# The written-out opening of a spectral-filter plus gated-MLP kernel, in another order

## The chip, the cores and the metric

One core of a Trainium2 chip runs the whole problem in one launch. Its engines are TensorE (PE: matmuls, with weight loads beside them), VectorE (DVE), ScalarE (ACT), GpSimd (POOL) and SyncE (SP), which issues the DMA transfers. Each takes its own instructions strictly in the order in which they stand in its queue, and waits at one until the semaphores that it names are reached. The metric is the device time of one execution in microseconds (us).

## The reference

The input `x` is 2048 tokens by 448 features, float32. The output is `x` plus two branches:

```python
xn = _layernorm(x, axis=-1)
A = irfft2(rfft2(xn) * (w_r + 1j * w_i))            # spectral filter over tokens and features
gate, up = x @ W_gate, x @ W_up                     # 448 -> 1792, here with xn for x
B = ((gate * (gate > 0)) * up) @ W_down             # 1792 -> 448
return x + A + B
```

Both branches take the normalised input `xn`.

## The kernel before

The tokens lie in 16 blocks of 128 (block n2), and four blocks make a chunk of 512: chunk 0 is blocks 0, 4, 8 and 12, chunk 2 is blocks 2, 6, 10 and 14. Every float32 operand of a matmul is split in two float16 parts, hi and lo, and a product is three matmuls (hi·hi, lo·hi, hi·lo). A block is normalised by DVE's bn_stats and bn_aggr, a reciprocal square root on ACT (`ln_sd`), three small DVE instructions that sharpen it (`ln_rstd`), and a fourth that makes the bias -mean·r. `ln_xn` writes the normalised block in float32 and `ln_hi` its hi part `tt`; `ln_copy` moves some columns on POOL, `ln_lo` subtracts on DVE. Then the block is transposed to the matmul layout `T`: in chunk 0 by TensorE (`ln_tp`, two groups of tiles a block, into PSUM) with a copy out of PSUM (`ln_ev`), in the other chunks by a transposing DMA (`ln_dma`).

The weights of gate and up come as slabs of 128 output features: slab (f, g), g = 0 gate, 1 up. A slab is loaded by DMA (256 KB, tile `wst`), its squares are summed on ACT (`w_sq`), POOL adds them over the partitions (`w_sum`), two small DVE instructions make a power of two of it (`w_scale`), ACT writes the hi part (`w_hi`) and DVE the lo part (`w_lo`), both into `wt`. A unit (f, chunk) is the 2x10 matmuls of both slabs of f with a chunk (`gu_full`), into two PSUM banks, and four matmuls of half the rows (`gu_halves`); then relu, product, and hi and lo parts of h (L799 to L811). Units of five f's are followed by the product with W_down (L834). The spectral branch is laid between them by a scheduler.

The first part, up to the first two units of chunk 2, is written out by hand: `OPENING` (L30 to L42) is a list of piece names, and each engine gets its instructions in the order in which the names stand. The names are a tag and a block or slab: `lx` load a block, `lw` load the next weight slab, `st` statistics, `sqA rsA` roots of blocks 0 and 4, `sqB rsB` of 8 and 12, `sqC rsC` of chunk 2; `ax` or `xn` normalise on ACT or DVE, `hi`/`hx` hi part from the raw or the normalised block, `cp`, `lo`; `tpA`/`tpB` transposes of a block, `vev`/`aev` the copy out of PSUM by DVE or ACT; `wsq par wsc whi wlo` the steps of a weight slab; `hh lh hl` (f = 0) and `ah bh ch` (f = 1) the matmuls of a slab with one half (256 columns) of chunk 0; `gu`, `hp` the later slabs and half-row matmuls; `re tm gh gl` the steps after a unit; `gz` slabs of chunk 2; `lwd wdq wdp wdsc wdh wdl` the W_down tiles; `warm` and `kw4` matmuls on zeros that nobody reads (`keep_warm`, 21 and 4 of them, 512 columns each).

SP's transfers use eight semaphores in turn, so one can be issued only when the eighth before it has landed.

Of the kernel before, what the change touches and what calls it, by code (L numbers as in the profile page):

```python
# [33 lines left out]
tpB12 wsqW3g0 vevB8 wloW1g0 ah10 wsqW3g1 vevB12 ah01 parW2 ah11 lwd2 wloW1g1 wscW2 bh00 hl11 hl01 lx14 whiW2g0
bh01 hp0 ch10 whiW2g1 lw st2 bh11 st6 re0 wloW2g0 bh10 wsqW4g1 ch00 ch11 tm0 gu2g0 parW3 wscW3 st14 wsqW4g0
whiW3g0 wloW2g1 ch01 ly0 parW4 wscW4 whiW3g1 wloW3g1 lw wsqW5g1 lx10 whiW4g0 wloW3g0 gh0 re1 st10 gu2g1 tm1 hp2
sqC rsC wsqW5g0 xn6 gu3g0 re2 parW5 wscW5 whiW5g0 tm2 wloW4g0 xn10 xn14 hx14 lwd4 hx6 lo6 hi10 whiW5g1 lo10
gu4g0 hx2 wloW5g0 whiW4g1 cp14 xn2 wdq0 gl0 cp10 gu3g1 wloW4g1 lo14 lwd3 wdq4 wdq2 cp2 re3 tm3 cp6 wloW5g1 gh1
# [106 lines left out]
def tile_gfnet_reglu(ctx: ExitStack, tc: tile.TileContext, x, xr, xi, wgu, wd, wf, c_fd, c_fm, c_im, c_row, c_id,  # L145
# [106 lines left out]
    def ln_stats(q, j):  # L252
        n2 = q + 4 * j
        st = ft([128, 6], F32, "bst", 2)
        V.bn_stats(st, xr_t[n2])  # L255
# [1031 lines left out]
```

## Time and profile before

| | us |
|---|---|
| median of 3 runs | 443.69 |
| lowest, highest | 442.72, 444.27 |
| span of the profiled execution, first to last instruction | 440.9 |
| PE busy in it | 435.7 |
| DVE, ACT busy in it | 382.3, 184.5 |

The profiled execution is known by its span alone. The runs' times hold what lies around the span too; their median is 2.8 us above it. A matmul's start is measured and its end is modelled: an own duration of 0.22 us stands for a matmul of 128 columns that lets the next one start after 0.06 us. So the pace is read from the starts.

### The profile page before, as it was taken

How to read it: one execution, taken by the hardware profiler on the slowest of the kernel's cores; microseconds unless marked ns; L12 is line 12 of the kernel's file. 1: busy time of each engine (PE TensorE's matmuls, PEld its weight loads, DVE VectorE, ACT ScalarE, POOL GpSimd, SP SyncE). 2: the span in 40 equal slices, each digit the busy share in tenths (PEclk: the TensorE clock that was granted, in tenths of full speed). 3: DMA queues.
4: the chain of work that ended last, by engine and by line, in shares of the span. 5: the costliest groups of instructions: out<-in, count | busy, mean ns of one | idle time of the engine just before them, and what ended most of it. 6: DMA issues, size and time to landing. Idle time of an engine off the chain costs nothing.

```text
span 440.9 us, 7429 instructions
## 1 busy us (share of the span) xinstructions
PE 435.7 (99%) x2641; PEld 221.9 (50%) x2641; DVE 382.3 (87%) x957; ACT 184.5 (42%) x396; POOL 29.4 (7%) x75
## 2 busy tenths in 40 slices
PE   8999999999999999999999999999999999999996
PEld 3744464554445545444545444444545555555664
DVE  6998496989887879999999999988997989798644
ACT  6995427392457236144023467233113332243220
POOL 3230002011100040000000020000000000000000
PEclk9999999999999999999999999999999999999999
DMA  7929895304111123332220210001111121210212
GB/s 256 301 91 198 269 364 172 70 2 107 59 49 50 47 76 119 94 118 84 86 84 1 84 43 1 0 1 42 44 43 49 54 91 34 72 55 33 89 51 104
DMA packets 37613, 39.55 MB, mean 90 GB/s; under 512 B 16535, under 2 KB 33353, under 8 KB 37577
## 3 DMA queue, kind: packets, MB, share of 16 engines
q1 hardware_dynamic: 37576, 39.09, 29.1%
q8 instruction: 20, 0.33, 0.3%
q14 instruction: 17, 0.13, 0.1%
HBM read 24.38 MB, written 3.67 MB: 64 GB/s over the span
## 4 chain that ended last, share of the span: by engine, by line
PE 90%; DVE 4%; ACT 3%; DMA 1%; issue 1%; SPq 0%; POOL 0%; ACTq 0%
PE bank L757 49%; PE bank L834 27%; PE bank L764 3%; PE fx L648 2%; PE fx L369 2%; PE fx L667 2%; PE fx L406 2%; PE bank L853 2%; ACT wt L699 1%; DMA T<-tt 1%; ACT junk L185 1%; DVE bst L255 1%; DVE wt L703 1%; DMA y<-in_xr 1%; ACT tt L304 1%
## 5 line engine op out<-in xcount | busy, mean ns | idle before, releaser
L757 PE MATMUL bank<-T,wt 128*128 128x512 f16 (+1 forms) x1160 | 252.7, 372 | 0.6 <-DVE T L345 0.5
L757 PEld LDWEIGHTS <-wt 128*128 128x128 f16 x1160 | 110.9, 98 | 127.6 <-issue 7.2
L834 PE MATMUL bank<-wdt,h 128*128 128x448 f16 x624 | 122.4, 352 | 0.0
L834 PEld LDWEIGHTS <-h 128*128 128x128 f16 x624 | 60.5, 98 | 55.1
L799 ACT ACTIVATE g<-bank 128x512 f32<-128x512 f32 x56 | 33.0, 591 | 80.4 <-PE bank L757 45.2
L807 ACT ACTIVATE h<-g 128x512 f16<-128x512 f32 x56 | 35.0, 627 | 70.1 <-DVE g L803 70.0
L803 DVE SCALAR_TENSOR_TENSOR g<-bank,g 128x512 f32<-128x512 f32 x56 | 38.2, 683 | 11.9 <-PE bank L757 6.8
L811 DVE TENSOR_TENSOR h<-g,h 128x512 f16<-128x512 f32 x56 | 38.1, 684 | 6.7 <-ACT h L807 6.4
L840 DVE SCALAR_TENSOR_TENSOR xy<-bank,dsc,xy 128x448 f32<-128x448 f32 x44 | 29.8, 676 | 5.5 <-PE bank L834 5.2
L632 ACT ACTIVATE vt<-y,fsc 128x456 f16<-128x456 f32 x15 | 10.1, 674 | 34.5 <-issue 14.0
L699 ACT ACTIVATE wt<-wst,wsc 128x512 f16<-128x512 f32 x28 | 19.3, 713 | 11.1 <-DVE wsc L195 10.3
L703 DVE SCALAR_TENSOR_TENSOR wt<-wst,wsc,wt 128x512 f16<-128x512 f32 x28 | 20.4, 742 | 0.5 <-ACT wt L699 0.3
L672 DVE SCALAR_TENSOR_TENSOR xy<-fx,fsc,xy 128x448 f32<-128x448 f32 x16 | 10.8, 680 | 10.9 <-PE fx L667 10.9
L188 POOL PARTITION_ALL_REDUCE wm<-wm x15 | 10.5, 697 | 139.9 <-ACT junk L185 136.4
L185 ACT ACTIVATE junk<-wst 128x512 bf16<-128x512 f32 x28 | 17.2, 616 | 0.0
L397 ACT ACTIVATE Xh<-X 128x456 f16<-128x456 f32 x16 | 9.3, 579 | 16.4 <-DVE X L395 9.3
L764 PE MATMUL bank<-T,wt 64*128 64x512 f16 x112 | 15.6, 380 | 0.0
L400 DVE TENSOR_TENSOR Xh<-X,Xh 128x456 f16<-128x456 f32 x16 | 9.8, 624 | 4.9 <-ACT Xh L397 4.9
L648 PE MATMUL fx<-im,vt 128*128 128x128 f16 x192 | 13.3, 219 | 0.0
L667 PEld LDWEIGHTS <-pgh 114*128 114x128 f16 x192 | 10.9, 98 | 3.8 <-issue 0.8
L648 PEld LDWEIGHTS <-vt 128*128 128x128 f16 x192 | 11.6, 98 | 1.3
L406 PE MATMUL fx<-Xh,fm 128*128 128x456 f16 x48 | 12.2, 356 | 0.0
(168 smaller groups left out, 480.1 us busy)
## 6 DMA issues: line engine op xcount, KB each, us to landing
wst<-in_wgu SPq DMA_DIRECT2D x28, 256.0 KB
sw<-y SPq DMA_DIRECT2D x56, 112.2 KB
wf<-in_wf SPq DMA_DIRECT2D x16, 228.0 KB
xy<-in_x SPq DMA_DIRECT2D x16, 224.0 KB
y<-in_xr SPq DMA_DIRECT2D x15, 224.0 KB
out<-xy SPq DMA_DIRECT2D x15, 224.0 KB
wdst<-in_wd SPq DMA_DIRECT2D x14, 224.0 KB
fm<-in_c_fm SPq DMA_DIRECT2D x4, 256.0 KB
```

Source lines behind the costliest of these rows:

```text
L185: A.activation(mt([128, 512], BF16, "junk", 2)[:, 0:src.shape[-1]], src, AF.Square, scale=SQ, accum_out=acc)
L648: P.matmul(o, v[:, h, w], m[:, c, :], start=(i == 0), stop=(i == 2), skip_group_check=True)
L699: A.activation(w[:, 0:4, :], wst[f, g], AF.Copy, scale=wsc[f, g])
L703: V.scalar_tensor_tensor(w[:, 4:8, :], st, sc, w[:, 0:4, :], op0=OP.mult, op1=OP.subtract)
L757: last["P"] = P.matmul(hps[f, q][g][:, cs], wt[f, g][:, a, :], Tq[q][:, b, cs], start=(start and i == 0), stop=(stop and i == len(seq) - 1 ...
L764: m = P.matmul(hps[f, q][g][:, 0:512], wt[f, g][rows, 7, :], Tq[q][rows, b, :], start=start, stop=stop).ins
L799: last["A"] = A.activation(g1s[f, q], hps[f, q][0], AF.Relu, scale=2.0 ** -22).ins
L803: last["V"] = V.scalar_tensor_tensor(g1, hps[f, q][1], 2.0 ** -22, g1, op0=OP.mult, op1=OP.mult).ins
L807: A.activation(ht[f, q][:, 0, :], g1s[f, q], AF.Copy)
L811: V.tensor_tensor(h[:, 1, :], g1s.pop((f, q)), h[:, 0, :], op=OP.subtract)
L834: last["P"] = P.matmul(ps[:, 0:D], ht[f, q][:, a, js], wdt[f][:, b, :], start=(i == 0), stop=(i == n - 1)).ins
L840: last["V"] = V.scalar_tensor_tensor(xy[:, n2, :], dps[n2][:, 0:D], dsc[:, g:g + 1], xy[:, n2, :], op0=OP.mult, op1=OP.add).ins
```

## The change

`OPENING` is written in another order, with a few new pieces, and the code gets what these need:

- `sq0 rs0`, `sq4 rs4`: blocks 0 and 4 have their roots apart, without the bias (`ln_bias`, pieces `nm0`, `nm4`, comes late); `rs` tiles have four buffers for three. Both blocks are normalised on DVE (`xn0`, `xn4`), and ACT makes the hi parts by a plain copy (`hx0`, `hx4`).
- `wsqW0g0` stands ahead of these copies on ACT, and `parW0g0 wscW0g0` follow early.
- The loads stand in another order: first the two blocks, slab W0g0, block 12, slabs W0g1 and W1g0, block 8. `fd_t` (`lfd`) comes among the first 12.
- The first unit's first half is done block by block: `hq lq kq` are 3, 3 and 4 matmuls of 128 columns; 40 matmuls of 128 columns stand for 20 of 256.
- Five of the eight copies out of PSUM are on ACT (`aevA0`, `aevB0`, `aevA8`, `aevA12`, `aevB8`).
- `vh8`, `vh12`, `vh6` make hi parts on DVE straight from the raw block, and `vwW2g0`, `vwW4g1` the hi parts of two weight slabs on DVE.
- The warming matmuls are 15 ahead of the transposes, 5 behind the first six transposes and 1 more.

```diff
-NWARM = 21
...
-OPENING = """lx0 st0 lx4 st4 sqA rsA ax4 hi0 lx8 st8 lx12 xn0 lw cp0 lw lw lw hx4 warm tpA4 st12 tpA0 lo0 lx6 sqB rsB cp4 lo4
-wsqW0g0 tpB0 kw4 tpB4 wsqW0g1 lx2 hi8 parW0g0 wscW0g0 lwd1 whiW0g0 vevA0 parW0g1 wscW0g1 vevA4 hh00 tpA8 whiW0g1
...
+OPENING = """lx0 lx4 lw st0 sq0 st4 sq4 rs0 wsqW0g0 rs4 lx12 xn0 hx0 parW0g0 xn4 wscW0g0 hx4 warm15 lw lw tpA0 st12 lo4 tpA4
+wsqW0g1 cp4 parW0g1 cp0 vevA4 lx8 warm5 tpB4 whiW0g0 aevA0 warm1 lw lo0 hq00 wloW0g0 tpB0 wsqW1g0 lq00 lwd4 wsqW1g1 lw
...
     def ln_sd(q, js=(0, 1, 2, 3)):
-        w = ft([128, 4, 4], F32, "rs", 3)
+        w = ft([128, 4, 4], F32, "rs", 4)
...
+    def ln_bias(q, js):
+        w, m = rsb[q, js[0]]
+        V.scalar_tensor_tensor(w[:, 3], m[:, :, 0], -1.0, w[:, 2], op0=OP.mult, op1=OP.mult)
...
-    def ln_hi(n2, fused=False):
+    def ln_hi(n2, fused=False, eng=None):
...
+        if eng is not None:
+            eng.tensor_scalar(o, xr_t[n2], mean, r, op0=OP.subtract, op1=OP.mult)
+        elif fused:
...
-    def w_hi(f, g):
+    def w_hi(f, g, eng=None):
...
+            eng.tensor_scalar(w[:, 0:4, :], wst[f, g], wsc[f, g], None, op0=OP.mult)
...
+                for j in range(2):
+                    for tag, sq in (("hq", seq1[0:3]), ("lq", seq1[3:6]), ("kq", seq2)):
+                        piece(f"{tag}{g}{j}", gu_full, f, q, (g,), slice(128 * j, 128 * j + 128), tag == "hq" and j == 0,
+                              False, sq)
```

ACT's queue behind its first instruction (`mv` statistics, `rs` roots, `wst` raw weights, `junk,wm` sums of squares, `wt` split weights, `y` and `tt` a block and its hi part, `T` the transposed chunk, `fx` a PSUM bank). Before:

```order
L266 ACTIVATE rs<-mv,eps 128x2
L295 ACTIVATE y_67<-g_127,rs 128x448
L304 ACTIVATE tt_100<-y_66,rs 128x448
L306 ACTIVATE tt_101<-y_67 128x448
L266 ACTIVATE rs<-mv,eps 128x2
L185 ACTIVATE junk,wm<-wst 128x512 x2
L304 ACTIVATE tt_102<-y_68,rs 128x448
L699 ACTIVATE wt<-wst,wsc 128x512 x2
L304 ACTIVATE tt_103<-y_69,rs 128x448
L185 ACTIVATE junk,wm<-wst 128x512 x2
```

Now:

```order
L265 ACTIVATE rs<-mv,eps 128x1 x2
L184 ACTIVATE junk,wm<-wst 128x512
L311 ACTIVATE tt_100<-y_68 128x448
L311 ACTIVATE tt_101<-y_69 128x448
L184 ACTIVATE junk,wm<-wst 128x512
L705 ACTIVATE wt<-wst,wsc 128x512
L348 ACTIVATE T_62<-fx 128x3x128
L184 ACTIVATE junk,wm<-wst 128x512 x2
L705 ACTIVATE wt<-wst,wsc 128x512
L348 ACTIVATE T_62<-fx 128x5x128
```

The two copies into `tt` are fed by DVE's blocks, the first sum of squares stands ahead of them and the second behind, and copies out of PSUM (L348) stand between the steps of the weights.

DVE's queue behind the statistics of blocks 0 and 4. Before:

```order
L258 BN_AGGR mv<-bst 128x2
L271 SCALAR_TENSOR_TENSOR rs<-mv,rs 128x2
L272 SCALAR_TENSOR_TENSOR rs<-rs 128x2
L273 SCALAR_TENSOR_TENSOR rs<-rs 128x2
L275 SCALAR_TENSOR_TENSOR rs<-mv,rs 128x2
L255 BN_STATS bst<-y_68 128x6
L258 BN_AGGR mv<-bst 128x2
L297 TENSOR_SCALAR y_70<-y_66,mv,rs 128x448
L255 BN_STATS bst<-y_69 128x6
L258 BN_AGGR mv<-bst 128x2
```

Now:

```order
L257 BN_AGGR mv<-bst 128x2
L270 SCALAR_TENSOR_TENSOR rs<-mv,rs 128x1
L271 SCALAR_TENSOR_TENSOR rs<-rs 128x1
L272 SCALAR_TENSOR_TENSOR rs<-rs 128x1
L270 SCALAR_TENSOR_TENSOR rs<-mv,rs 128x1
L271 SCALAR_TENSOR_TENSOR rs<-rs 128x1
L272 SCALAR_TENSOR_TENSOR rs<-rs 128x1
L300 TENSOR_SCALAR y_68<-y_66,mv,rs 128x448
L300 TENSOR_SCALAR y_69<-g_123,mv,rs 128x448
L190 TENSOR_SCALAR eg<-wm 128x1
L194 TENSOR_SCALAR wsc<-eg 128x1
```

Two sets of roots, one column wide each, stand where one set of two columns stood; both blocks follow at once, then the scale of the first slab and block 12's statistics.

SP's queue from its start (`in_xr`, `in_xi` blocks, `in_wgu` weight slabs, `in_wd` W_down). Before:

```order
L225 DMA y_66<-in_xr 128x448
L220 DMA g_127<-in_xi 128x512
L225 DMA y_68<-in_xr 128x448
L225 DMA y_69<-in_xr 128x448
L231 DMA wst<-in_wgu 128x512 x4
L225 DMA y_71<-in_xr 128x448
L225 DMA y_72<-in_xr 128x448
L241 DMA wdst<-in_wd 128x448
L214 DMA xy<-in_x 128x448
L231 DMA wst<-in_wgu 128x512 x6
```

Now:

```order
L224 DMA y_66<-in_xr 128x448
L219 DMA g_123<-in_xi 128x512
L230 DMA wst<-in_wgu 128x512
L224 DMA y_67<-in_xr 128x448
L230 DMA wst<-in_wgu 128x512 x2
L224 DMA y_70<-in_xr 128x448
L230 DMA wst<-in_wgu 128x512
L240 DMA wdst<-in_wd 128x448
L230 DMA wst<-in_wgu 128x512 x2
L1104 DMA fd_t<-in_c_fd 128x912
L230 DMA wst<-in_wgu 128x512 x2
L224 DMA y_71<-in_xr 128x448
```

The first weight slab is the third transfer for the fifth, the second slab is the fifth for the sixth.

## Rows read from the trace of the kernel before

**Rows 1.** The page: busy time of each engine, share of the span; PEclk by slice.

```profile
PE 435.7 (99%) x2641; PEld 221.9 (50%) x2641; DVE 382.3 (87%) x957; ACT 184.5 (42%) x396; POOL 29.4 (7%) x75
...
PEclk9999999999999999999999999999999999999999
```

**Rows 2.** The page: the chain that ended last, share by engine.

```profile
PE 90%; DVE 4%; ACT 3%; DMA 1%; issue 1%; SPq 0%; POOL 0%; ACTq 0%
```

**Rows 3.** Waits of PE: engine, line, released by: us in total, times, longest.

```profile
PE bank L757 <- DVE T L345: 0.5, 1, 0.5
```

**Rows 4.** Timeline of PE: start us, us, engine, line, operation, tiles, count.

```profile
1.22 7.46 PE L1094 MATMUL bank<-row_t 128*128 128x512 f16 x21 [1.22 <-DVE row_t L1166]
...
7.22 1.46 PE L1094 MATMUL bank<-row_t 128*128 128x512 f16 x6
...
8.52 0.78 PE L337 MATMUL fx<-g,tt 128*128 128x128 f16 x11
9.13 1.03 PE L1094 MATMUL bank<-row_t 128*128 128x512 f16 x4
9.99 0.44 PE L337 MATMUL fx<-g,tt 128*128 128x128 f16 x5
10.93 0.49 PE L757 MATMUL bank<-T,wt 128*128 128x256 f16 x3 [0.49 <-DVE T L345]
11.25 0.33 PE L337 MATMUL bank<-g,tt 128*128 128x128 f16 x3
11.52 0.94 PE L757 MATMUL bank<-T,wt 128*128 128x256 f16 x7
...
26.41 8.81 PE L757 MATMUL bank<-T,wt 128*128 128x512 f16 x40
```

**Rows 5.** Timeline of SP's queue.

```profile
8.01 0.33 SPq L231 DMA_DIRECT2D wst<-in_wgu  x1
```

**Rows 6.** Timeline of ACT.

```profile
7.34 0.56 ACT L306 ACTIVATE tt<-y 128x448 f16<-128x448 f32 x1
...
8.13 0.61 ACT L185 ACTIVATE junk<-wst 128x512 bf16<-128x512 f32 x1
...
8.74 0.61 ACT L185 ACTIVATE junk<-wst 128x512 bf16<-128x512 f32 x1
...
10.13 1.33 ACT L699 ACTIVATE wt<-wst,wsc 128x512 f16<-128x512 f32 x2
```

**Rows 7.** Timeline of DVE.

```profile
4.70 0.18 DVE L258 BATCH_NORM_AGGREGATE mv<-bst 128x2 f32<-128x6 f32 x1
5.24 0.16 DVE L271 SCALAR_TENSOR_TENSOR rs<-mv,rs 128x2 f32<-128x2 f32 x1 [0.36 <-ACT rs L266]
...
5.90 0.62 DVE L255 BATCH_NORM_STATS2 bst<-y 128x6 f32<-128x448 f32 x1
...
6.66 0.48 DVE L297 TENSOR_SCALAR y<-y,mv,rs 128x448 f32<-128x448 f32 x1
```

**Rows 8.** Groups by form, ACT then DVE: count, busy us, mean ns.

```profile
L699 ACT ACTIVATE wt<-wst,wsc 128x512 f16<-128x512 f32 x12 | 8.2, 712 | 0.9 <-DVE wsc L195 0.7
...
L799 ACT ACTIVATE g<-bank 128x512 f32<-128x512 f32 x10 | 5.7, 584 | 3.9 <-PE bank L764 3.9
...
L382 ACT ACTIVATE zc<-fx 128x228 f32<-128x228 f32 x4 | 1.4, 360 | 5.9 <-PE fx L369 5.9
...
L345 DVE COPY T<-fx 128x640 f16<-128x640 f16 x3 | 1.4, 479 | 0.0
L345 DVE COPY T<-fx 128x384 f16<-128x384 f16 x3 | 1.0, 348 | 0.0
```

**Rows 9.** SP's transposing DMAs, the chain there (start, us), PE at its end.

```profile
33.71 4.88 SPq L330 DMA_TRANSPOSE T<-tt  x3
...
36.42 3.87 DMA T<-tt
...
39.62 1.10 PE L757 MATMUL bank<-T,wt 128*128 128x512 f16 x3
```

More of the change, by code (lines that the diff above doesn't have):

```diff
@@ L34 @@
[L34 to L38, printed above, removed]
@@ L39 @@
-gu4g1 gh2 wdq3 ly12 lo2 hp4 wdq1 wdp wdsc wdh4 dm10 gl1 re4 ly8 wdh3 gl2 gu5g1 tm4 gh4 dm14 gl4 dm6 gu5g0 dm2
-re5 lfd gz0g0 wdl3 gz0g1 tm5 hp6 gh3 gl3 rz0 gh5 wdl4 gl5 wdh1 wdl1 wdh2 wdl2 n0 wdh0 wdl0 gz1g0 tz0 gz1g1 rz1
-hz0 tz1 hz1 lz0 lz1
+OPENING = """lx0 lx4 lw st0 sq0 st4 sq4 rs0 wsqW0g0 rs4 lx12 xn0 hx0 parW0g0 xn4 wscW0g0 hx4 warm15 lw lw tpA0 st12 lo4 tpA4
+wsqW0g1 cp4 parW0g1 cp0 vevA4 lx8 warm5 tpB4 whiW0g0 aevA0 warm1 lw lo0 hq00 wloW0g0 tpB0 wsqW1g0 lq00 lwd4 wsqW1g1 lw
+lq01 wscW0g1 hq01 vevB4 st8 whiW0g1 kq01 parW1 aevB0 hq10 hq11 lw sqB lfd wscW1 kq11 wloW0g1 lw rsB lw lx10 kq10 kq00
@@ new lines @@
+lq11 whiW1g1 whiW1g0 lq10 ah10 ly12 vh8 vh12 ch10 cp12 cp8 wloW1g0 tpA8 ax8 lwd2 lw aevA8 ah00 tpA12 lw aevA12 wsqW2g1
+wsqW2g0 wsqW3g1 xn12 ch00 bh00 hh01 lh11 lo8 lx14 tpB8 ah01 parW2 lo12 aevB8 wloW1g1 tpB12 vevB12 bh01 lh01 lwd0
+wsqW3g0 wscW2 st14 hh11 vwW2g0 lx6 lx2 wdq0 parW3 hl01 hl11 st10 wloW2g0 st6 wscW3 ah11 hp0 bh10 bh11 wsqW4g1 ch11
+ch01 re0 lw lw st2 whiW2g1 wsqW5g1 wsqW4g0 whiW3g0 tm0 wsqW5g0 wloW2g1 re1 wloW3g0 parW4 parW5 tm1 gu2g0 whiW3g1 sqC
+wloW3g1 rsC wscW5 gh0 xn10 xn2 hx2 wscW4 lwd3 gu2g1 lwd1 ly0 hp2 hx14 gl0 whiW4g0 re2 ly8 ax14 whiW5g1 hi10 whiW5g0
@@ L42 @@
+lo2 vwW4g1 gu3g0 tm2 gu3g1 wloW4g0 cp2 wloW4g1 gh2 vh6 wloW5g1 re3 lo10 wloW5g0 wdq3 cp10 gh1 lo14 wdq4 tm3 ax6 n0
+gu4g0 gh3 gu4g1 gl1 hp4 wdq1 gu5g1 cp14 lo6 dm2 re4 cp6 gu5g0 ly4 wdq2 wdp gl2 nm4 wdsc dm10 wdh2 re5 dm14 tm4 gh4 tm5
+dm6 wdh4 gz0g0 gl3 gz0g1 wdh3 hp6 wdl3 gz1g0 wdh0 gl4 wdl4 gz1g1 rz0 tz0 wdh1 hz0 rz1 nm0 wdl1 lz0 wdl2 wdl0 tz1 gh5
+hz1 gl5 lz1
 """
@@ L255, in ln_stats @@
         V.bn_stats(st, xr_t[n2])
-        if j == 0:
+        if q not in mv:
             mv[q] = ft([128, 4, 2], F32, "mv", 2)
         V.bn_aggr(mv[q][:, j, :], st)
-    rst = {}
+    rst, rsb = {}, {}
     def ln_sd(q, js=(0, 1, 2, 3)):
-        w = ft([128, 4, 4], F32, "rs", 3)
+        w = ft([128, 4, 4], F32, "rs", 4)
         n = len(js)
-        rst[q, js[0]] = w[:, :, 0:n], mv[q][:, js[0]:js[-1] + 1, :]
-        A.activation(w[:, 0, 0:n], rst[q, js[0]][1][:, :, 1], AF.Abs_reciprocal_sqrt, bias=eps)
+        rsb[q, js[0]] = w[:, :, 0:n], mv[q][:, js[0]:js[-1] + 1, :]
+        A.activation(w[:, 0, 0:n], rsb[q, js[0]][1][:, :, 1], AF.Abs_reciprocal_sqrt, bias=eps)
     def ln_rstd(q, js=(0, 1, 2, 3), bias=False):
-        w, m = rst[q, js[0]]
+        w, m = rsb[q, js[0]]
         r0, t, r, nm = (w[:, i] for i in range(4))
@@ L274, in ln_rstd @@
         if bias:
-            V.scalar_tensor_tensor(nm, m[:, :, 0], -1.0, r, op0=OP.mult, op1=OP.mult)
+            ln_bias(q, js)
         for i, j in enumerate(js):
             rst[q, j] = r[:, i:i + 1], nm[:, i:i + 1], m[:, i, 0:1]
+    def ln_bias(q, js):
+        w, m = rsb[q, js[0]]
+        V.scalar_tensor_tensor(w[:, 3], m[:, :, 0], -1.0, w[:, 2], op0=OP.mult, op1=OP.mult)
     xn, tt, xn_b = {}, {}, {}
@@ L297, in ln_xn @@
             V.tensor_scalar(xn[n2], xr_t[n2], mean, r, op0=OP.subtract, op1=OP.mult)
-    def ln_hi(n2, fused=False):
+    def ln_hi(n2, fused=False, eng=None):
         new_tt(n2)
         o = tt[n2].rearrange("p a b -> p (a b)")[:, 0:D]
-        r, nm, _ = rst[n2 % 4, n2 // 4]
-        if fused:
+        r, nm, mean = rst[n2 % 4, n2 // 4]
+        if eng is not None:
+            eng.tensor_scalar(o, xr_t[n2], mean, r, op0=OP.subtract, op1=OP.mult)
+        elif fused:
             A.activation(o, xr_t[n2], AF.Identity, scale=r, bias=nm)
@@ L695, in w_scale @@
             wsc[f, k] = sc[:, i:i + 1]
-    def w_hi(f, g):
+    def w_hi(f, g, eng=None):
         w = wt[f, g] = mt([128, 8, 128], F16, "wt", 2 * NR + 4)
-        A.activation(w[:, 0:4, :], wst[f, g], AF.Copy, scale=wsc[f, g])
+        if eng is None:
+            A.activation(w[:, 0:4, :], wst[f, g], AF.Copy, scale=wsc[f, g])
+        else:
+            eng.tensor_scalar(w[:, 0:4, :], wst[f, g], wsc[f, g], None, op0=OP.mult)
     def w_lo(f, g):
@@ L1096, in tile_gfnet_reglu @@
     pieces = {"lfd": lambda: nc.sync.dma_start(fd_t, c_fd),
-              "lw": load_wn, "warm": lambda: keep_warm(NWARM),
-              **{f"kw{n}": (lambda n=n: keep_warm(n)) for n in (1, 3, 4)},
+              "lw": load_wn, **{f"warm{n}": (lambda n=n: keep_warm(n)) for n in range(1, 25)},
               "wdp": lambda: wd_sum(len(groups[0])),
@@ L1110, in tile_gfnet_reglu @@
             n2 = q + 4 * j
+            piece(f"sq{n2}", ln_sd, q, (j,))
+            piece(f"rs{n2}", ln_rstd, q, (j,))
+            piece(f"nm{n2}", ln_bias, q, (j,))
             for tag, fn, *a in (("lx", load_xr), ("ly", load_x), ("st", ln_stats, j), ("xn", ln_xn),
-                                ("hi", ln_hi, c == 0), ("hx", ln_hi, c == 1), ("ax", ln_xn, True), ("cp", ln_copy), ("lo", ln_lo), ("dm", ln_dma),
+                                ("hi", ln_hi, c == 0), ("hx", ln_hi, c == 1), ("ax", ln_xn, True), ("cp", ln_copy), ("lo", ln_lo),
+                                ("vh", ln_hi, False, V), ("dm", ln_dma),
                                 ("tpA", ln_tp, (0, 1, 2)), ("tpB", ln_tp, (4, 5, 6, 3, 7))):
@@ L1151, in tile_gfnet_reglu @@
             piece(f"whiW{f}g{g}", w_hi, f, g)
+            piece(f"vwW{f}g{g}", w_hi, f, g, V)
             piece(f"wloW{f}g{g}", w_lo, f, g)
```

2 lines of the change are left out of this document (removed).

## The prediction

> **What bounds the kernel now.** I read the busy times first. PE is busy for 435.7 of 440.9 us; DVE, the next, has 13% to spare [rows 1]. The chain that ended last says the same from the other side: 90% of it is PE [rows 2]. PE's waits come third: beside its start they list a single wait for data, 0.5 us, in the opening [rows 3]. So PE is a belt that runs nearly without a hole from the first matmul to the end. A reordered opening can only move the belt's start, the holes near it, and the useless matmuls on it. What it saves or loses there arrives at the end one for one, unless something holds PE later.
>
> PE's timeline shows that start [rows 4]. 21 warming matmuls begin at 1.22. The last six begin at 7.22 and hand over at 8.52, so they stand 0.217 us apart. The first fifteen took 6.00 us, 0.40 apart. 512 columns in 0.217 us is the 2.4 GHz level, and the early ones ran at 1.2 GHz although the PEclk row shows full clock throughout [rows 1]; the rise falls near 7.0. Transposes follow at 8.52 (eleven in 0.78, of which the last one's own duration is 0.22: 0.056 us a piece), four more warming matmuls, five transposes at 9.99, and the first real matmul at 10.93.
>
> **The change part by part,** on the time axis of the profiled execution. It is known by its span of 440.9 us, 2.8 us below the median of the runs; I carry a difference in the span over to the median.
>
> *Start of the transposes.* Fifteen warming matmuls end at 7.22, where the sixteenth began before [rows 4]. Are the data there? DVE has the statistics of both blocks at 4.88 [rows 7]. Four root instructions took 5.24 to 5.90, 0.165 each; six take 0.99, so both roots stand at 5.87. Two normalisations at 0.48 give 6.35 and 6.83, and two hi copies on ACT at 0.56 [rows 6] give about 6.95 and 7.5. ACT's first sum of squares stands ahead of these copies and waits for the third transfer, which before had landed by 5.90, since the block it carried was read then without a wait [rows 7]. It fits in front of 6.6 or costs a tenth or two. So the first transposes start at 7.22 for 8.52: **-1.30 us**.
>
> *Warming matmuls behind that.* Four before, six now, at 0.217: **+0.43 us**.
>
> *Holes.* Before: five transposes from 9.99 end at 10.27 and PE restarts at 10.93, 0.66; three from 11.25 end at 11.42 with a restart at 11.52, 0.10. Together 0.76 [rows 4].
> After: ACT decides them. Its second sum of squares needs slab W0g1, the fifth transfer. SP's thirteenth transfer reuses the fifth one's semaphore and waited for it until 8.01 [rows 5]. The new fifth has 32 KB more ahead of it; I keep 8.0. From there ACT runs without a pause: squares 0.61 (8.13 to 8.74 [rows 6]), hi part of W0g0 0.62 (two in 1.33 [rows 6], one's own 0.71 [rows 8]), and the copy of block 0 out of PSUM. ACT did no such copy before. From PSUM it took 0.360 for 228 columns and 0.584 for 512 [rows 8]; a straight line gives 0.48 for 384 and 0.69 for 640. That ends at 9.75, and the first real matmul comes at 9.8 for 10.93. Then two sums of squares (1.22) and W0g1's hi part (0.71) end at 11.7, and the second copy of block 0 at 12.3.
> PE's work between: transposes until 7.39, a hole of 0.1 until block 4's hi part, three transposes and five warming matmuls until 8.75, five transposes and one warming matmul until 9.25, hole 0.55. From 9.8 there are 21 instructions of 128 columns, 1.18 us, until 10.98; hole 0.72 until W0g1's hi part at 11.7. Ten more until 12.26, hole 0.1 until the second copy. Fourteen more, 0.78, meet W1g1's hi part at 13.1 (two more ACT instructions behind 12.3). From there the stock of work is as large as before. Sum 1.5: **+0.74 us**.
>
> *Blocks of 128 columns.* 40 at 0.056 are 2.24 us; 20 of 256 at 0.11 (seven in 0.94, the last one's own 0.27 [rows 4]) are 2.2. Nothing.
>
> *Loads, roots' bias, hi parts on DVE.* `fd_t` comes 30 us earlier and is first needed far behind; SP's queue ahead of slab W0g1 is one load shorter. The biases go to where chunk 2's DVE work has room. Five copies of 0.35 to 0.48 us leave DVE [rows 8] and five hi parts of about 0.48 [rows 7] come to it, beside two more sets of roots, one block that ACT normalised and two that ACT takes over: nothing in sum, hidden under PE.
>
> The opening comes to -1.30 + 0.43 + 0.74 = **-0.13 us**.
>
> *The next lock.* Chunk 2's first slab waits for its fourth transposing DMA. SP issued the last three one behind the other from 33.71; the fourth, at 36.42, landed 3.87 us later, at 40.29 [rows 9]. PE's row shows it: three matmuls that should stand 0.216 apart (forty in 8.81, the last one's own 0.38 [rows 4]) and end after 0.81 took 1.10 [rows 9]. So 0.29 us is lost here, which the wait list, made from modelled ends, leaves out. PE would be here at 40.05, now at 39.92. The fourth transpose comes earlier only if block 6 does, whose hi part and subtraction stand at the end of DVE's work of equal length, while its three predecessors now leave earlier, so SP is free when it comes. I take 0.3 earlier, landing at 40.0; the ends are 0.7 earlier (half of the 1.36 us between two of the three issues, 33.71 to 36.42 [rows 9]) and 0.5 later than before (one DVE hi part more ahead of it). The slab starts at the later of 39.92 and 40.04: 40.05 for 40.34, **-0.29 us** in all.
>
> 443.69 - 0.29 = **443.4 us**. Bounds of the unknown costs: the two copies on ACT between DVE's 0.35 and 0.48 and twice the 0.584 of the 512-column read, -0.34 to +1.2; W0g1's landing between 7.5 and 8.6, -0.5 to +0.6; the fourth transpose -0.4 to +0.8 against my value.
>
> The copies are where a rule speaks against the change. The Trainium skill, "ScalarE: Activation LUTs", section "Rules for kernel authors", budgets about 0.3 us an ACTIVATE and 0.83 ns an element. By it the two copies would be 0.62 and 0.83 for my 0.48 and 0.69, the opening would come to +0.15, and the kernel to about 443.7. The trace has 0.360 for 228 columns where the rule makes 0.49, so I stay with the rows.
>
> **The rivals.**
>
> *ACT's queue is the new bound, and the kernel is slower.* Place: ACT from 8.0 to 13.1, seven steps in a row without slack, ahead of everything PE can do. For it: the order now puts squares that wait for a DMA ahead of a finished slab's hi part and of a copy that PE needs. Against it: before, ACT had as many steps there. Every tenth on ACT is a tenth on PE, and it decides once the seven steps end 0.42 us later than worked out, from where PE starts the slab behind 40.34. With W0g1 at 8.6 (+0.6) and both copies half as long again (+0.6), PE comes to the slab at 41.1: +0.8 against before, **444.5**.
>
> *The clock isn't up.* Before, the rise to 2.4 GHz fell near 7.0 and six more dense matmuls followed [rows 4]. Now the warming run ends at 7.22, and a third of the time until 12.3 is holes. If the rise comes behind it, or the clock falls back to 1.2 GHz, the 3.0 us of work from 8.75 to 13.1 double, of which 1.4 us fall into the holes: +1.6 on the opening, PE at the slab at 41.5, and **444.9**; a rise as late as that from 7.22 on costs 1.4 more, a short relapse half. Against it: PE is as busy until 7.0 as before, and a hole of 0.66 left the pace alone. The Trainium skill, "TensorE: Matmul & The Clock Gate", Part 1, says that the number of cold matmuls at a start varies between runs of one kernel; by that rule fifteen could be too few in some runs and not in others. One trace can't show this.
>
> *The holes close and the transposes land early.* W0g1 at 7.5 shortens the opening by 0.5, the copies at DVE's speed by 0.3; PE is at the slab at 39.1, and the transposes, 0.7 earlier, at 39.6: -0.7 to -1.0, **442.8**.
>
> *It does what it says and it doesn't matter*, since a later wait takes the gain: 443.7, inside the forecast.
>
> **How the numbers follow.** Forecast with that last case 0.62 (443.0 to 443.9), holes closed 0.16 (442.2 to 443.0), ACT 0.15 (443.9 to 445.0), clock 0.07 (444.3 to 446.3). A measurement of this kernel can tell about 0.3%, 1.33 us, from no change: its three runs lie 1.55 us apart. Below 442.36 falls most of half of the second case and a share for a median that is itself uncertain by about 0.5: 0.13. Above 445.02 fall half of the clock case, the end of the ACT case and the same share of the median's: 0.10. The range 442.4 to 444.8 leaves out one in ten at either end.
>
> **What would show it.** Right: transposes at 7.2, the first matmul of 128 columns at 9.8, holes near 9.3 and 11.0 behind ACT's hi parts and copies, no hole behind 13.2, and PE at chunk 2's first slab at 40.0 with little or no pause. Wrong: matmuls of 128 columns 0.11 us apart behind 7.2 (clock); ACT waiting for slab W0g1 beyond 8.2; DVE copies ending first; or the slab of chunk 2 starting after 40.3 for a transposing DMA. The prediction as a whole fails if PE has holes behind 45 us, where it had none.

## The result, and the profile after

The changed kernel takes 444.85 us (median of 7 runs, 443.48 to 445.33) beside 442.77 for the kernel before (7 runs, 442.6 to 444.27): a ratio of 1.0034, 95% interval 1.0022 to 1.0047. By the ratio it is slower by about 1.5 us (the medians alone lie 2.1 us apart), where 443.4 was forecast, and just above the end of the range.

The page of the changed kernel has the same shape as before, with a little less PE and more of other engines in the chain that ended last:

```profile
span 442.6 us, 7463 instructions
PE 434.7 (98%) x2657; PEld 221.7 (50%) x2657; DVE 382.4 (86%) x960; ACT 184.5 (42%) x398; POOL 32.6 (7%) x75
...
PE 80%; DVE 9%; DMA 5%; ACT 2%; issue 1%; SPq 1%; POOL 1%; DVEq 0%; ACTq 0%
```

PE is busy for 1.0 us less than before [rows 1]: its warming takes 1.7 us less (21 matmuls for 25, and more of them at the faster pace), all else 0.7 more. And yet the span is 1.7 us longer. So 2.7 us of new holes have to be found. POOL, of which the prediction said nothing, is busy for 32.6 us where it was 29.4. PE's list now has six waits behind the opening's first, where there was one [rows 3]; the four longest are:

```profile
PE bank L342 <- POOL tt L316: 1.1, 1, 1.1
PE bank L765 <- DMA T<-tt: 0.8, 1, 0.8
PE fx L342 <- ACT tt L311: 0.6, 1, 0.6
PE bank L772 <- DVE g L811: 0.4, 1, 0.4
```

The timeline of PE, against [rows 4], shows the opening close to the forecast until 16, and then the first of them:

```profile
1.23 5.12 PE L1102 MATMUL bank<-row_t 128*128 128x512 f16 x15 [1.23 <-DVE row_t L1182]
6.91 0.81 PE L342 MATMUL fx<-g,tt 128*128 128x128 f16 x6 [0.57 <-ACT tt L311]
...
9.48 0.33 PE L765 MATMUL bank<-T,wt 128*128 128x128 f16 x3
...
15.90 0.39 PE L342 MATMUL bank<-g,tt 128*128 128x128 f16 x4
17.42 0.23 PE L342 MATMUL bank<-g,tt 128*128 128x128 f16 x1 [1.14 <-POOL tt L316]
...
26.86 0.61 PE L772 MATMUL bank<-T,wt 64*128 64x512 f16 x4
```

Four transposes of block 8 run at 15.90; the fifth, of tile 7, waits until 17.42. From one start to the next, less the 0.054 us that 128 columns take, 1.31 us are lost. Tile 7 is what POOL fills with two small copies. Here are POOL's four copies for blocks 12 and 8, first before, then after:

```profile
13.72 0.31 POOL L310 COPY tt<-tt 128x48 f16<-128x48 f16 x1
13.96 0.23 POOL L311 COPY tt<-tt 128x64 f16<-128x64 f16 x1
14.14 0.22 POOL L310 COPY tt<-tt 128x48 f16<-128x48 f16 x1
14.30 0.23 POOL L311 COPY tt<-tt 128x64 f16<-128x64 f16 x1
```

```profile
14.22 0.68 POOL L315 COPY tt<-tt 128x48 f16<-128x48 f16 x1 [2.87 <-DVE tt L307]
14.84 1.71 POOL L316 COPY tt<-tt 128x64 f16<-128x64 f16 x1
16.48 0.70 POOL L315 COPY tt<-tt 128x48 f16<-128x48 f16 x1
17.13 0.23 POOL L316 COPY tt<-tt 128x64 f16<-128x64 f16 x1
```

They start 0.5 us later and take 3.1 us in place of 0.8. The same instructions, the same 48 and 64 columns. What is new stands on DVE, which runs beside them without a gap:

```profile
13.22 0.93 DVE L307 TENSOR_SCALAR tt<-y,mv,rs 128x448 f16<-128x448 f32 x2
14.07 0.75 DVE L711 SCALAR_TENSOR_TENSOR wt<-wst,wsc,wt 128x512 f16<-128x512 f32 x1
14.73 0.51 DVE L300 TENSOR_SCALAR y<-y,mv,rs 128x448 f32<-128x448 f32 x1
15.15 0.55 DVE L326 TENSOR_TENSOR tt<-y,tt 128x384 f16<-128x384 f32 x1
15.62 0.22 DVE L327 TENSOR_TENSOR tt<-y,tt 128x64 f16<-128x64 f32 x1
15.76 0.55 DVE L326 TENSOR_TENSOR tt<-y,tt 128x384 f16<-128x384 f32 x1
16.23 0.22 DVE L327 TENSOR_TENSOR tt<-y,tt 128x64 f16<-128x64 f32 x1
16.36 0.74 DVE L711 SCALAR_TENSOR_TENSOR wt<-wst,wsc,wt 128x512 f16<-128x512 f32 x1
```

The first copy ends with the first L711, the third with the second L711; the second sits through five DVE instructions. The fourth, with DVE idle behind 17.1, takes its usual 0.23.

The other two new holes stand far behind the opening. PE had none there before, except for the pause of 0.29 us at 40 [rows 9]. That pause is gone: the half-row groups on either side of it are 9.28 us apart (36.14 and 45.42) where they were 9.56. But then:

```profile
80.73 0.21 PE L374 MATMUL fx<-fd_t,Tl 128*128 128x114 f16 x1
81.75 1.24 PE L765 MATMUL bank<-T,wt 128*128 128x512 f16 x5 [0.81 <-DMA T<-tt]
...
203.29 0.82 PE L772 MATMUL bank<-T,wt 64*128 64x512 f16 x6 [0.38 <-DVE g L811]
```

Before, the same place:

```profile
80.07 0.21 PE L369 MATMUL fx<-fd_t,Tl 128*128 128x114 f16 x1
80.25 1.02 PE L757 MATMUL bank<-T,wt 128*128 128x512 f16 x4
```

0.97 us are lost at 80.73 (before: 0.13) and 0.54 in front of 203.29 (before: 0.10). Compared instruction by instruction, PE stands 0.99 us behind the kernel before at the half-row groups of 26.86, 0.66 behind at 50, 1.50 behind at 81.75 and 1.94 behind at 203.29, and that is what is left at the end. So half of the loss, 0.99 us, is the opening's; the pause of 40 that is gone gives back 0.33; and 0.84 and 0.44 come near 80 and 203, where the change touches nothing.

At 80 PE waits for chunk 1's fourth transposing DMA. The trace's DMA records give each one's issue and its last landing, and the packets of queue 8, which the page lists as "instruction" (21 of them, 16 KB each; PE has 2657 matmuls and as many weight loads, so that is one for about 253 PE instructions):

```
chunk 1's transposing DMAs, issue -> last landing (us)           fetch: start, us
before  73.13->75.95  74.62->77.37  76.01->78.74  77.41->80.11   60.0 0.99, 81.4 0.97
after   71.78->75.11  75.02->79.98  76.48->80.81  77.87->81.61   59.6 1.09, 77.6 0.92
chunk 2's last three
before  33.71->36.43  35.06->39.27  36.42->40.28                 36.2 1.42
after   34.08->36.84  35.45->38.20  37.12->39.83                 33.9 0.93
```

A transposing DMA of this table that no fetch disturbs lands 2.7 to 3.3 us after its issue (2.7 to 3.8 in all twelve traces). Only where a fetch starts while one is under way does it take 4 us or more, and those behind it wait: before at 36.2, after at 77.6. Overlap alone is not enough: after's fetch at 33.9 was still under way when the DMA of 34.08 was issued, and that one took 2.8 us; so did three in the kernels below where the fetch began within 0.06 us of the issue. Two more things are different there: SP now issues two small transfers between the first and the second DMA of chunk 1, and DVE's order from 58 to 78 us is another, since the scheduler took over from another state. The fetch and SP's order are thus rivals, and have to be told apart.

### The profile page after: what moved, and what is told of

Same layout as the page of the kernel before. It is cut to its first block, busy times and chain, and to the rows that moved or that the text cites. A ratio compares the mean times of both kernels' runs of the same rounds, so it can differ in the third digit from the quotient of the medians.

```text
span 442.6 us, 7463 instructions
## 1 busy us (share of the span) xinstructions
PE 434.7 (98%) x2657; PEld 221.7 (50%) x2657; DVE 382.4 (86%) x960; ACT 184.5 (42%) x398; POOL 32.6 (7%) x75
## 4 chain that ended last, share of the span: by engine, by line
PE 80%; DVE 9%; DMA 5%; ACT 2%; issue 1%; SPq 1%; POOL 1%; DVEq 0%; ACTq 0%
PE bank L765 45%; PE bank L842 22%; PE bank L772 3%; PE fx L653 2%; DMA wst<-in_wgu 2%; PE fx L672 2%; PE bank L861 2%; PE fx L411 2%; PE fx L374 2%; DMA T<-tt 1%; DVE xy L848 1%; DMA sw<-y 1%; DMA wf<-in_wf 1%; DVE g L811 1%; DMA sw<-yx 1%
## 5 line engine op out<-in xcount | busy, mean ns | idle before, releaser
L765 PE MATMUL bank<-T,wt 128*128 128x512 f16 (+2 forms) x1180 | 253.0, 368 | 1.2 <-DMA T<-tt 0.8
L811 DVE SCALAR_TENSOR_TENSOR g<-bank,g 128x512 f32<-128x512 f32 x56 | 38.2, 684 | 12.7 <-PE bank L765 7.0
L705 ACT ACTIVATE wt<-wst,wsc 128x512 f16<-128x512 f32 x26 | 18.1, 711 | 10.7 <-DVE wsc L194 9.4
L187 POOL PARTITION_ALL_REDUCE wm<-wm x15 | 11.6, 772 | 139.7 <-ACT junk L184 136.2
L711 DVE SCALAR_TENSOR_TENSOR wt<-wst,wsc,wt 128x512 f16<-128x512 f32 x28 | 20.4, 744 | 1.0 <-ACT wt L705 1.0
L387 ACT ACTIVATE zc<-fx 128x228 f32<-128x228 f32 x16 | 5.7, 357 | 17.2 <-PE fx L374 17.0
```

What stands on the lines that cost most here:

```text
L711: V.scalar_tensor_tensor(w[:, 4:8, :], st, sc, w[:, 0:4, :], op0=OP.mult, op1=OP.subtract)
L765: last["P"] = P.matmul(hps[f, q][g][:, cs], wt[f, g][:, a, :], Tq[q][:, b, cs], start=(start and i == 0), stop=(stop and i == len(seq) - 1 ...
L811: last["V"] = V.scalar_tensor_tensor(g1, hps[f, q][1], 2.0 ** -22, g1, op0=OP.mult, op1=OP.mult).ins
```

## The experiments

Ten kernels ran. "Before" stood beside all of them, at 443.04, 443.03 and 442.95 us in three sessions. None of them changes the order of any other instruction on any engine than its edit names.

**The copies off POOL.** Theory A: DVE's instructions hold POOL's copies up, and PE waits for them. Rival B: the late start of the hi parts is to blame. Rival C: later locks swallow the opening.

```
-... vh8 vh12 ch10 cp12 cp8 wloW1g0 ...
-... lo8 lx14 tpB8 ah01 parW2 lo12 aevB8 ...
+... vh8 vh12 ch10 wloW1g0 ...
+... lo8 vc8 lx14 tpB8 ah01 parW2 lo12 vc12 aevB8 ...    (vc: the same two copies, on DVE)
```

> The same four copies on DVE, block 8's right behind its subtraction and block 12's behind its own; the rest unchanged. Theory A: four copies of 0.1 to 0.25 us on DVE, tile 7 of block 8 is ready near 16.2 and DVE's later subtraction is 0.3 later; PE's pause at 16.1 is 0.5 or less in sum with what follows at block 12, PE 0.7 to 1.2 us earlier at 27 us. Rival B: pause above 0.9. Rival C: the pause goes and the time of the kernel stays within 0.2 us of after's.

Measured: 443.86 us, ratio to before 1.0016 (1.0006 to 1.0025). The pause is gone, and the five transposes of block 8 stand in one row:

```profile
15.86 0.44 PE L342 MATMUL bank<-g,tt 128*128 128x128 f16 x5
...
16.50 0.54 PE L342 MATMUL fx<-g,tt 128*128 128x128 f16 x5
...
26.21 0.61 PE L772 MATMUL bank<-T,wt 64*128 64x512 f16 x4 [0.45 <-DVE wt L711]
```

PE is 1.32 us earlier than after at the second row of transposes (16.50 for 17.82) and 0.65 earlier at 26: the copies cost DVE 0.09 us each from start to start, and DVE, which has no room until 26, hands them on to the lo part of a slab. At 80 it pauses for 0.94 us as after does. A holds, B falls.

The other way, with all four on ACT behind its second eviction:

```
-... aevA12 wsqW2g1 ...
+... aevA12 ac8 ac12 wsqW2g1 ...    (ac: the two copies on ACT; cp12 cp8 taken out)
```

> The four small copies of blocks 8 and 12 move from POOL to ACT, behind ACT's second eviction (15.1 us); every other engine keeps its instructions and their order. Theory A (POOL is held up by DVE's instructions on SBUF operands, and PE waits for POOL): four copies of 0.2 to 0.3 us on ACT end near 16.1, PE's pause of 1.3 us at 16.1 shrinks to 0.4 or less and PE is 0.9 to 1.3 us earlier at 27 us; the whole kernel is 0.3 to 1.3 us faster than after, less if a transposing DMA holds PE at 80 us as before. Rival B (the pause comes from the late hi parts, not from POOL): the copies cannot start earlier than on POOL and PE's pause stays above 0.9. Rival C (the opening's delay is swallowed by later locks): the pause goes and the time of the kernel stays within 0.2 us of after's.

Measured: 443.94 us, 1.0019 (1.0010 to 1.0029). The pause at 16 is gone here too; the four copies delay ACT's eviction of block 8 and PE loses 0.43 us at 18.5. In the profiled execution the opening began 0.8 us later than in after's, so PE stood at 26.83 as in after: its row of transposes waited for ACT, which stood in front of a sum of squares until the third transfer landed at 6.50 (5.65 in after's trace). So one trace of the opening can mislead by that much; a median over 12 runs misleads less.

**DVE steps aside.** The copies stay on POOL and start as late as after's; one small DVE instruction that reads their result makes DVE wait for them.

```
-... cp12 cp8 wloW1g0 ...
+... cp12 cp8 lk8 wloW1g0 ...    (lk8: DVE copies 8 columns of block 8's tile 7 to a spare tile)
```

> The copies stay on POOL and start as late as in after, but DVE now waits in between: one small DVE instruction that reads what the last copy of block 8 wrote stands ahead of DVE's next long ones. Theory A (DVE's SBUF traffic holds POOL): the four copies take 0.22 to 0.3 us each, about 0.8 in all instead of 3.1, and DVE loses about 0.9 us in waiting; PE's pause then stands behind block 8's subtraction instead, 0.7 to 1.2 us in sum. Rival B (these copies are slow by themselves, or by their late start): they take about 3 us here too, and PE's pause grows to over 3 us.

```profile
14.27 0.22 POOL L315 COPY tt<-tt 128x48 f16<-128x48 f16 x1 [3.07 <-DVE tt L307]
14.42 0.24 POOL L316 COPY tt<-tt 128x64 f16<-128x64 f16 x1
14.60 0.22 POOL L315 COPY tt<-tt 128x48 f16<-128x48 f16 x1
14.76 0.24 POOL L316 COPY tt<-tt 128x64 f16<-128x64 f16 x1
```

```profile
15.03 0.17 DVE L1123 CAST ed<-tt 128x8 f32<-128x8 f16 x1 [0.83 <-POOL tt L316]
```

This settles it: the same copies at the same time take 0.22 to 0.24 us when DVE is still. The price moves to DVE (0.83 us of waiting) and from there to PE, which loses 0.97 us at 14.9 behind a slab's lo part; I had put that pause behind block 8's subtraction. One run took 444.18.

**The fetches moved.** Fifteen warming matmuls of 512 columns are written as sixty of 128. That is the same number of columns, and 90 instructions more ahead of everything. Theory D: the fetch makes the pause at 80. Rival E: SP's order makes it.

```
-        for _ in range(n):
-            P.matmul(wps, warm[:, 0:128], warm, start=True, stop=True)
+        for a, b in [(128 * k, 128 * k + 128) for k in range(4)] * (15 if n == 15 else 0) + [(0, 512)] * (n - (15 if n == 15 else 0)):
+            P.matmul(wps[:, a:b], warm[:, 0:128], warm[:, a:b], start=True, stop=True)
```

> The first fifteen warming matmuls of 512 columns are each written as four of 128: the same columns, 90 instructions more on PE ahead of everything else; no engine's order changes. What moves is where PE's instruction fetches fall: 16 KB each, 256 instructions, so each comes some 5 to 8 us earlier, the one at 77.6 to about 70. Theory D (a fetch that falls into chunk 1's transposing DMAs holds them up): the second transposing DMA lands at most 3.2 us after its issue for 5.0, PE's pause of 0.97 us at 80.7 falls to 0.3 or less, and the kernel is 0.5 to 0.9 us faster than after. Rival E (SP's new order of issues makes the pause): the DMA lands as late as in after, or the pause stays above 0.7 us; time as after, within 0.3 us. The pause of 1.3 us at 16.1 stays in both.

Measured: 443.34 us, 1.0005 (0.9997 to 1.0014). The fetch of 77.6 came at 69.0, and with SP's order unchanged the four transposing DMAs landed 3.3, 2.8, 2.7 and 2.7 us after their issues. PE at 81:

```profile
81.06 0.21 PE L374 MATMUL fx<-fd_t,Tl 128*128 128x114 f16 x1
81.11 1.24 PE L765 MATMUL bank<-T,wt 128*128 128x512 f16 x5
```

No pause, against 0.97; 1.31 us are lost at 16.4 as ever, and the loss at 202 is 0.13 for 0.54. D holds, E falls. The gain is larger than expected, and the hole at 202 shows why. In after, DVE waits 1.4 us for a transfer sw<-y near 185, beside a fetch at 183.5, and runs without a gap from there until PE wants its result at 203. With the fetch elsewhere it waits 1.0 us; first after, then the split:

```profile
DVE y L558 <- DMA sw<-y: 1.4, 1, 1.4
```

```profile
DVE y L558 <- DMA sw<-y: 1.0, 1, 1.0
```

**The mirror.** If a fetch makes the pause, it can be given to the kernel before, whose SP has the old order. Eight of its 21 warming matmuls are split: 48 instructions more, nothing else.

```
-        for _ in range(n):
+        for a, b in [(128 * k, 128 * k + 128) for k in range(4)] * (8 if n == 21 else 0) + [(0, 512)] * (n - (8 if n == 21 else 0)):
```

> The kernel before, with eight of its 21 warming matmuls written as four of 128 columns: 48 PE instructions more at the start, no order changed, no work added. PE's fetch at 36.2 moves to about 32.5, the one at 81.4 to 76 to 78, into chunk 1's transposing DMAs. Theory D: the pause of 0.28 us at 39.8 goes, and a new pause of 0.5 to 1.8 us stands at 80 us, with a transposing DMA that lands 4 us or more after its issue; the kernel becomes 0.2 to 1.5 us slower. Rival E (SP's order of issues is what makes after's pause; before has the old order): no pause above 0.3 at 80, time as before or 0.3 us faster.

Measured: 443.60 us, 1.0013 (1.0003 to 1.0022). The fetch of 81.4 came at 74.2, earlier than the 76 to 78 I expected, and fell on the first two DMAs, which landed 4.3 and 3.9 us after their issues. SP, held up behind them, took 6.37 us over four issues; below it PE at 80:

```profile
73.19 6.37 SPq L330 DMA_TRANSPOSE T<-tt  x4
```

```profile
80.13 0.21 PE L369 MATMUL fx<-fd_t,Tl 128*128 128x114 f16 x1
81.18 1.02 PE L757 MATMUL bank<-T,wt 128*128 128x512 f16 x4 [0.84 <-DMA T<-tt]
```

The kernel before now has after's pause: 1.00 us are lost. Its own pause at 39.8 is gone, since the fetch of 36.2 came at 30.1. 48 useless instructions, at no cost in PE time, take one pause away and make another. By the two pauses, 1.00 against 0.28, it should lose 0.7 us; the medians lie 0.57 apart.

**Both repairs.** Block 8's copies go to DVE, block 12's to ACT, and the warming is split. To make room, one sum of squares (`wsqW3g1`) goes behind ACT's last copy out of PSUM.

```
-... aevA12 wsqW2g1 wsqW2g0 wsqW3g1 ... lo8 lx14 ... lo12 aevB8 ...
+... aevA12 ac12 wsqW2g1 wsqW2g0 ... lo8 vc8 lx14 ... lo12 aevB8 wsqW3g1 ...    (and cp12 cp8 out, fifteen split)
```

> Both repairs at once: after with block 8's two copies on DVE behind its subtraction, block 12's two on ACT ahead of a sum of squares that nothing waits for soon, and the fifteen warming matmuls split in four. Theory A and D together: no pause above 0.4 us near 16, none above 0.3 at 80, none above 0.2 at 202; PE stands 1.0 to 1.4 us earlier than after at 27 us, and the kernel takes 442.0 to 442.9, which is 0.2 to 1.0 us faster than before. If the opening's gain is swallowed by chunk 2's or chunk 1's transposing DMAs (rival C), it takes what the kernel with the split alone took, 443.1 to 443.6.

Measured: 442.67 us, 0.9993 (0.9982 to 1.0004), the fastest of all by its median, 2.2 us below after by medians of two sessions, 1.8 by the ratios to before, and from before not to be told apart. No pause behind 13 is above 0.17 us:

```profile
16.02 0.44 PE L342 MATMUL bank<-g,tt 128*128 128x128 f16 x5
...
25.79 0.61 PE L772 MATMUL bank<-T,wt 64*128 64x512 f16 x4
...
49.22 0.92 PE L842 MATMUL bank<-wdt,h 128*128 128x448 f16 x4
```

All four copies on DVE, and the split (the edits of the first and the fourth kernel together):

> All four copies on DVE, as in the earlier run, and the split. Theory A and D: the pause of 0.94 us at 80.1 goes as it did for the split alone; the pause of 0.61 at 25.4, which DVE's work made, stays; 442.5 to 443.3, that is 0.5 to 1.4 us faster than the copies on DVE alone. Rival C: within 0.3 us of the copies on DVE alone.

Measured: 442.85 us, 0.9992 (0.9980 to 1.0004), 1.0 us below the copies on DVE alone; no pause at 80, 0.58 us lost at 26 as expected.

The first repair without the second:

> The copies of blocks 8 and 12 off POOL as in the kernel with both repairs, the warming matmuls unsplit, so that PE's fetches fall as in after: near 77 and 183. Theory A and D: no pause above 0.4 us near 16, a pause of 0.6 to 1.1 us at 80 with the second transposing DMA landing 4 us or more after its issue; 443.4 to 444.0, that is 0.8 to 1.4 us below after and 0.7 to 1.3 above the kernel with both repairs. If the copies off POOL are all that matters, 442.4 to 443.0 and no pause at 80.

Measured: 443.57 us, 1.0010 (1.0001 to 1.0020). No pause at 16; a fetch at 75.8 struck the second DMA (4.9 us) and held SP's third issue for 2.67 us. PE's waits:

```profile
PE bank L765 <- DMA T<-tt: 1.5, 1, 1.5
```

That is 1.6 us lost at 80, more than expected, and 0.5 and 0.6 at 189 and 203. The split is worth 0.9 us beside the repaired copies by the medians, 0.75 by the ratios to before.

**The opening's start.** ACT's sum of squares of W0g0, which waits for the third transfer, goes behind block 0's hi part.

```
-... rs0 wsqW0g0 rs4 lx12 xn0 hx0 ...
+... rs0 rs4 lx12 xn0 hx0 wsqW0g0 ...    (on top of both repairs)
```

> As the kernel with both repairs, and ACT's sum of squares of slab W0g0, which waits for the third transfer, stands behind block 0's hi part instead of ahead of it. Theory F (this wait makes the opening's start vary by up to 0.9 us between runs): the first transposes come at 6.8 to 7.0 in this run whatever the third transfer does, block 4's 0.3 to 0.5 later, and the kernel takes 0 to 0.5 us less than the one with both repairs. Rival G: the scale of W0g0, and with it the first real matmul, comes later by a hi part, and the kernel takes 0.2 to 0.6 us more.

```profile
6.88 0.34 PE L342 MATMUL fx<-g,tt 128*128 128x128 f16 x3
7.95 0.34 PE L342 MATMUL fx<-g,tt 128*128 128x128 f16 x3 [0.74 <-ACT tt L311]
...
10.07 0.44 PE L342 MATMUL fx<-g,tt 128*128 128x128 f16 x5 [0.70 <-DVE T L350]
```

Measured: 443.35 us, 1.0003 (0.9994 to 1.0013). The transposes do start at 6.88, and everything behind them is late: 0.7 us slower than with the order of after. Rival G holds; the change's order was the better one here.

**The changed kernel once more,** for a second trace.

> The changed kernel itself, unchanged, beside the others for a second trace and a second set of times. If the account holds, POOL's four copies take about 3 us again with DVE running back to back, PE's pause near 16 is 1.2 to 1.4 us, that at 80 is 0.6 to 1.1 and that at 202 is 0.3 to 0.7; 444.3 to 445.0. If these pauses were chance of the one trace, at least one of them is missing or half as long.

Measured: 444.43 us, 1.0033 (1.0021 to 1.0046). 1.31 us are lost at 16.6, for the third time to a hundredth, with the same four copies (0.68, 1.71, 0.70, 0.23). At 81 it is 1.47, and at 203 only 0.15. The fetch fell at 76.9 and the second DMA took 4.95 us; near 185 DVE waited 1.1 us for its transfer instead of 1.4. So the first pause is the program's, the same each time; the later two vary between executions, the one at 80 by half and the one at 203 to under a third, which by the expectation above counts as chance of the one trace. Their sum was 1.51 and 1.62.

## Why the prediction was wrong

*Where it failed.* The step on "loads, roots' bias, hi parts on DVE", which closed with "nothing in sum, hidden under PE". It weighed DVE's time and PE's cover and left out what DVE's instructions do to POOL. The hi parts of blocks 8 and 12 on DVE make its work dense just when POOL has its copies, and PE has only 2 us of other work in front of tile 7. The price is 1.31 us at 16, in all three traces that keep the copies on POOL beside a busy DVE. By medians it is 0.7 to 0.9 us: 443.34 to 442.67 with the split, 444.43 to 443.57 without (by the ratios to before, 0.5 and 1.0); what the copies and the moved sum of squares cost on DVE and ACT is in these numbers too. Where the median fell was partly luck: the second set of runs of the same kernel, 444.43, lies inside the range of 442.4 to 444.8. The slowdown is what the forecast missed.

The rows to see it in were there. In the trace of before, POOL's copies last 0.22 to 0.24 us, or until a scaling, a subtraction or a lo part that DVE is working on ends. Here is one that was held, and what DVE did:

```profile
32.40 0.73 POOL L311 COPY tt<-tt 128x64 f16<-128x64 f16 x1
```

```profile
32.30 0.74 DVE L703 SCALAR_TENSOR_TENSOR wt<-wst,wsc,wt 128x512 f16<-128x512 f32 x1
```

And one that was not, from the trace of after, POOL first and then DVE; one of DVE's inputs, fx, lies in PSUM:

```profile
72.31 0.22 POOL L315 COPY tt<-tt 128x48 f16<-128x48 f16 x1 [0.58 <-ACT tt L311]
```

```profile
72.14 0.62 DVE L459 TENSOR_TENSOR y<-y,fx 128x456 f32<-128x456 f32 x1
```

The Trainium skill, "SBUF — State Buffer", section "Who interferes with whom", states this rule: a DVE instruction with two inputs in SBUF contends with a GpSimd instruction that reads SBUF, the first to issue keeps the shared interface for its whole instruction, and the other is blocked, not slowed. The traces agree (L711 0.68 and 0.70, L459 0.22). Two inputs are not all, though: in the trace of after, a TENSOR_SCALAR (L307), with one block and two columns of scalars as inputs, held the copy at 32.21 for 0.49 us, while BN_STATS (7.26 to 7.88) did not hold the one at 7.39, 0.22. By the rule as it stands a copy waits for one instruction; here one waited through five, 1.71 us. The page should have been a rival of the prediction, with a chance.

*The second failure is a term that the sum didn't have.* "The prediction as a whole fails if PE has holes behind 45 us, where it had none": it has. The 128-column blocks cost "nothing" in PE time, and that is so, but the new program has 16 more matmuls and as many more weight loads, 32 PE instructions, and so the fetches fall elsewhere. The one at 81.4 became 77.6, in the middle of four transposing DMAs on which PE has no slack. What it is worth by medians: 0.90 (443.57 to 442.67), 1.01 (443.86 to 442.85) and 1.1 to 1.5 (after to the split alone), by the ratios to before 0.75, 1.1 and 1.3; put into the kernel before, 0.57 on the other side. The Trainium skill, "Runtime: NRT & Kernel Launch", section "Instruction fetch mechanics", describes a sequencer that fetches blocks of 16 KB over its own DMA queue and calls the cost of a crossing mostly hidden. The size is what the trace shows. The cost is hidden from the engine that fetches (behind 18 us PE loses no more than its usual 0.1 us at after's other fetches, but for what follows the one of 183.5), and not from a transfer that is under way: 2.7 us became 3.8 to 5.0.

*The next lock, -0.29:* it came, to a hundredth, and for another reason. I expected the fourth transposing DMA to be issued 0.3 earlier. It was issued 0.70 later (37.12 for 36.42) and flew 1.15 shorter, and PE itself came 0.95 later (36.14 for 35.19 at the half-row group), which would all but have hidden the pause anyway (37.12 and 3.87 make 40.99; PE was due at 41.0). The pause in the kernel before had itself been a fetch, at 36.2: the mirror, and both repairs with PE at 35.07, have no such fetch and no pause. The row with 3.87 us from issue to landing [rows 9] stood beside two others of 2.7 and 4.2, and I didn't ask why they differ.

*What held.* ACT's copies out of PSUM took 0.48 to 0.49 and 0.68 to 0.70 us for the 0.48 and 0.69 of the straight line; an estimate by the rule in the Trainium skill ("ScalarE: Activation LUTs", section "Rules for kernel authors") would have had 0.62 and 0.83. (The prediction's aside on that rule doesn't add up: with +0.15 for the opening PE would be at chunk 2's slab at 40.20, which makes 443.55, not 443.7.) The transposes started at 6.91 (7.22 worked out), the first real matmul came at 9.48 (9.8), and PE lost 1.66 us in six pauses from there until 12.7 (1.5 forecast). One term was off: slab W0g1, kept at 8.0 with 7.5 as the lower bound, landed at 7.43; ACT and PE were both earlier than worked out, so that the pauses came out is in part luck. With both causes taken out, PE stands 0.12 us ahead of before at the half-row group of 35 (35.07 for 35.19) and 0.40 ahead at 49.2 (49.22 for 49.62). The sum had said 0.13 and 0.42. So close a fit is luck: the first repair alone, with the same opening, has 35.42 and 49.56, since its transposes began 0.34 later (7.38 for 7.04). The terms that were in the sum are borne out to some 0.3 us.

*The rivals.* ACT's queue did not decide. The clock came up earlier, not later: from the first matmul at 1.23 on PE ran dense in both traces, and its matmuls of 512 columns stand 0.43 us apart (the 1.2 GHz level) until 4.6 and 0.22 (2.4 GHz) from 4.9 on, where the kernel before got there near 7.0; the fifteen took 4.95 us from start to start for 6.00. It gained nothing, since the hi parts came at 6.9. Nor is it the order's doing: in the other traces that open with these fifteen in one piece the rise came between 4.2 and past 7.2, and in the latest of them (all copies on DVE) the first real matmul still came at 9.44. No rival had POOL or the fetches. The chance of a time above 445.02, 0.10, was put on ACT and the clock; a mechanism that the rows spoke for got none.

*Open:* why the pause at 203 is 0.54 and 0.61 in some traces and 0.13 to 0.15 in others is told above by a fetch beside one transfer. The traces fit: where that fetch started between 183.29 and 183.50, 0.54 to 0.61 us were lost (four traces), at 182.80 and 184.45 0.11 and 0.15. But no kernel moved that fetch alone, so this is not shown. How a fetch holds up a transposing DMA, on its queue, its ring or on the way, no run here shows.

## What to carry to other kernels

When work is moved to an idle-looking engine, look at who shares its memory path: beside a DVE that is dense with scalings and subtractions in SBUF, a 0.2 us copy on POOL was as long as what DVE was doing, or longer, and if PE needs it next, it belongs on another engine. When a kernel waits for a transfer with no slack, compare the flights of equal transfers first; if one is 2 us longer than its sisters, look for an instruction fetch in the DMA records. And an edit that only adds instructions moves all later fetches, so a difference of 0.2% far from an edit may be a fetch that fell elsewhere: add a few instructions ahead of everything, and see whether it goes.

## What the runs showed of the hardware that was not expected

- POOL's copy of 64 columns took 0.23 us alone, 0.49 beside one TENSOR_SCALAR (L307), up to 0.73 beside one DVE instruction with two SBUF inputs, and 1.71 behind five in a row (three traces); it doesn't always get the next turn.
- A fetch of 16 KB, 0.9 to 1.8 us by its packet, made transposing DMAs last 3.8 to 5.0 us instead of 2.7 to 3.8 (most 2.7 to 2.9), in eight traces, and held SP's next issue for up to 2.76 us instead of 1.23.
- Programs with the same first transfers open differently: the third landed between 5.45 and 6.50 us, and with ACT waiting for it the first transposes started between 6.91 and 7.77.
